# Packed q for the first 512 tokens, weights in 256-column chunks, and a first output stage by chunks of f over four PSUM tiles

## The chip, the core and the metric

The kernel runs on one core of one Trainium2 chip. TensorE (PE) does the matmuls, with its weight loads (PEld) beside them; VectorE (DVE), ScalarE (ACT) and GpSimd (POOL) do elementwise work; SyncE (SP) issues all DMA transfers, in program order. Each engine works through its own instruction list in order and waits on semaphores. Matmul results land in PSUM, eight banks of 128 partitions x 2 KB; all else lives in SBUF, 128 partitions wide. The metric is the device time of one execution, in microseconds; less is better.

## The reference

Decayed linear attention in blocks, four batches, eight heads, 768 tokens, head dimension 64, and then a bilinear feed-forward over the 3072 tokens:

```python
for b in range(nb):
    intra = np.einsum('bhic,bhjc->bhij', qb, kb) * Dmask[None]
    intra = np.einsum('bhij,bhjd->bhid', intra, vb)
    inter = np.einsum('bhid,bhde->bhie', qb * lam_pow[None], kv_state)
    out[:, :, sl] = intra + inter
    kv_state = lam_block[None, :, None, None] * kv_state + np.einsum('bhsd,bhse->bhde', kb_dec, vb)
x = np.ascontiguousarray(attn_out.transpose(0, 2, 1, 3)).reshape(B * S, H * D)   # 3072 x 512
a = x @ w_a          # 512 x 1536
b = x @ w_b          # 512 x 1536
return (a * b @ w_out).astype(np.float32)                                       # 1536 x 512
```

All inputs and the output are float32; the kernel multiplies in bfloat16 and accumulates in float32.

## The kernel before

**Units and groups.** The 3072 tokens are 24 units of 128 tokens (6 units to a batch, `NB = 6`). Units are gathered in groups of `GROUPS = (4, 2, 4, 4, 4, 4, 2)`. The attention of a unit writes 128 columns of its group's `xT` (512 features on 4 x 128 partitions, up to 512 tokens); then `ffn` runs over the group.

**The attention of a unit** is cut in pieces. `prep` scales q and k by powers of lambda (`lp_q`, `lp_k`, made at the start from `lam`) into the bf16 tile `qk` and casts v to `vb`. T (`piece_T`) transposes `qk` on PE into `tps`, eight 128x128 transposes, and copies it to `qkT` on ACT. From unit 10 on (`DMA_T_FROM = 10`) a DMA transpose that SP issues in `prep` fills `qkT` instead. K (`scores`, `masks`) makes the 8 score matrices `kq` and multiplies them by a triangular mask on DVE into `m`. O (`piece_O`) adds the state's part (`o_ps` from `st` and `qkT`) and the masked scores' part (`o_ps` from `m` and `vb`), copies `o_ps` to `xT` on ACT, adds the unit's k and v to the state (`kvd`) and copies the state to `st` on DVE. X is O of a unit with K of the next one inside it.

**ffn** first runs over the 12 chunks f of 128 hidden features: four matmuls into `a_ps` (L306), a copy to `a_sb` on ACT (L309), four matmuls into `b_ps` (L312), and the product `ab` on DVE (L314). Then, for each unit t of the group, 12 matmuls into `op` (L319), a copy to `o_sb` on ACT and a store (L325).

**Hooks.** After each f, and twice in each t, `ffn` calls `hook(slot)`; slots 0 to 11 are the f, 12 and up the halves of the t. The hook emits the next group's attention pieces at the slots that `piece_plan(g)` lists, so PE has them between matmuls of the present group. There is no scheduler: the order of emission is the order on every engine.

**Weights and loads.** `w_a` and `w_b` come in column chunks of 256, 256, 512 and 512 (`W_CHUNKS`), `w_out` in three chunks of 512 rows (o0, o1, o2), all into the staging tiles `wst` (6 buffers), and are cast to bf16 on DVE (`w_a`), ACT (`w_b`) and POOL or DVE (`w_out`). The q, k and v of a unit are three loads of 256 KB in rows of 256 bytes; six units may be loaded ahead (`LOOKAHEAD`). `prefetch` issues them from the hook. SP's order is: `lam`; q, k, v of units 0 to 3 with the first `w_a` and `w_b` chunks between; the other `w_a` and `w_b`; `w_out`; units 4 and 5; then the units one by one, with the stores and DMA transposes where the hooks emit them. The framework lets eight transfers be outstanding: each waits for the one eight places ahead of it.

**The start** (L337 to L351) runs prep and T of unit `step`, K of the unit before and O of the one before that, for six steps, ahead of the first `ffn`. PSUM tiles rotate through seven banks (`ps_bank`); the eighth holds the state.

Of the kernel before, what the change touches and what calls it, by code (L numbers as in the profile page):

```python
# [28 lines left out]
W_CHUNKS = (256, 256, 512, 512)  # L29
LOOKAHEAD = 6  # L30
DMA_T_FROM = 10


def piece_plan(g):

    if g + 1 == len(GROUPS):
        return {}
    if g == 0:  # L40
        ps = [("T", 0, 14), ("K", 0, 15), ("T", 1, 15), ("O", 0, 17), ("K", 1, 17), ("O", 1, 18)]
    elif g == 1:
        ps = [("T", 0, 1), ("K", 0, 3), ("O", 0, 5), ("T", 1, 6), ("K", 1, 8), ("T", 2, 10),
              ("O", 1, 10), ("K", 2, 11), ("O", 2, 12), ("T", 3, 13), ("K", 3, 14), ("O", 3, 15)]
    elif GROUPS[g + 1] == 2:
        ps = [("T", 1, 3), ("X", 0, 5), ("O", 1, 11)]
    else:
        ps = [("T", 1, 2), ("X", 0, 4), ("T", 2, 7), ("X", 1, 9), ("T", 3, 11), ("X", 2, 13),
              ("T", 4, 15), ("X", 3, 17)]
        if g == 2:  # L50
            ps = [("T", 0, 0), ("K", 0, 2)] + ps
    plan = {}
    for name, k, s in ps:
        plan.setdefault(s, []).append((name, k))
    return plan
# [3 lines left out]
def kernel(  # L59
# [19 lines left out]
    assert sum(GROUPS) == NU  # L79
# [5 lines left out]
    wst_pool = ctx.enter_context(tc.tile_pool(name="wst", bufs=6))  # L85
# [4 lines left out]
    st_pool = ctx.enter_context(tc.tile_pool(name="st", bufs=2))  # L90
# [4 lines left out]
    ps_pool = ctx.enter_context(tc.tile_pool(name="ps", bufs=7, space=PSUM))  # L95
# [4 lines left out]
    def ps_bank(name, shape, dt):  # L100
        return ps_pool.tile(shape, dt, name=name, tag="ps")
# [7 lines left out]
    def load_unit(u, which="qkv"):  # L109
        b, nb = divmod(u, NB)  # L110
        for w in which:
            t = ld_pool.tile([128, H, D], F32, name=w + "f", tag=w + "f")
            nc.sync.dma_start(out=t, in_={"q": qr, "k": kr, "v": vr}[w][b, nb])  # L113
            raw[u, w] = t
# [7 lines left out]
    w_off = [sum(W_CHUNKS[:i]) for i in range(len(W_CHUNKS) + 1)]  # L122
    staged = {}

    def load_w(kind, c):
        w = W_CHUNKS[c] if kind != "o" else 512
        t = wst_pool.tile([128, 4, 512], F32, name="wst", tag="wst")
        if kind == "o":
            nc.sync.dma_start(out=t, in_=wo_r[:, 4 * c:4 * c + 4, :])
        else:  # L130
            r = wa_r if kind == "a" else wb_r
            nc.sync.dma_start(out=t[:, :, :w], in_=r[:, :, w_off[c]:w_off[c] + w])
        staged[kind, c] = t

    def cast_w(kind, c, eng):
        t = staged.pop((kind, c))
        if kind == "o":
            dst, src = wo_sb[:, 4 * c:4 * c + 4, :], t
        else:
            w = W_CHUNKS[c]  # L140
            dst = (wa_sb if kind == "a" else wb_sb)[:, :, w_off[c]:w_off[c] + w]
            src = t[:, :, :w]
        if eng == "act":
            nc.scalar.copy(dst, src)
        elif eng == "dve":
            nc.vector.tensor_copy(dst, src)
        else:
            nc.gpsimd.tensor_copy(dst, src)  # L148
# [4 lines left out]
    load_unit(0)  # L153
    load_unit(1)
    load_unit(2, "qk")
    load_unit(3, "qk")
    load_w("a", 0)
    load_unit(2, "v")
    load_unit(3, "v")
    load_w("b", 0)  # L160
    for c in (1, 2):
        load_w("a", c)
        load_w("b", c)
# [4 lines left out]
    gpos = singles.tile([128, NB], F32, name="gpos")  # L168
    nc.gpsimd.iota(gpos, pattern=[[BLK, NB]], base=1, channel_multiplier=1,
# [11 lines left out]
    tmpe = singles.tile([128, NB, H], F32, name="tmpe")  # L181
    lp_q = singles.tile([128, NB, H, 1], F32, name="lp_q")
    lp_k = singles.tile([128, NB, H, 1], F32, name="lp_k")
    nc.vector.tensor_mul(tmpe, _bc(loglam, [loglam.ap[0], [0, NB], loglam.ap[1]]),
                         _bc(gpos, [gpos.ap[0], gpos.ap[1], [0, H]]))
    nc.scalar.activation(lp_q[:, :, :, 0], tmpe, AF.Exp)
    nc.scalar.activation(lp_k[:, :, :, 0], tmpe, AF.Exp, scale=-1.0)
# [7 lines left out]
    def prep_v(u, early):  # L195
        vb = prep_pool.tile([128, H, D], BF16, name="vb", tag="vb")
        vf = raw.pop((u, "v"))
        if early:
            nc.scalar.copy(vb, vf)
        else:  # L200
            nc.vector.tensor_copy(vb, vf)  # L201
        U[u]["vb"] = vb

    def prep(u, early=False):
        nb = u % NB
        qf, kf = raw.pop((u, "q")), raw.pop((u, "k"))
        qk = prep_pool.tile([128, 2, H, D], BF16, name="qk", tag="qk")
        lq = lp_q[:, nb].to_broadcast([128, H, D])
        lk = lp_k[:, nb].to_broadcast([128, H, D])
        (nc.vector if early else nc.gpsimd).tensor_mul(qk[:, 0], qf, lq)  # L210
        nc.gpsimd.tensor_mul(qk[:, 1], kf, lk)  # L211
        U[u] = dict(qk=qk)
        if not early:
            prep_v(u, False)
        if u >= DMA_T_FROM:
            qkT = qkT_pool.tile([128, 2, HP, 128], BF16, name="qkT", tag="qkT")
            nc.sync.dma_start_transpose(out=qkT[:].rearrange("p j hp i -> p (j hp) i"),
                                        in_=qk[:].rearrange("p j h d -> p (j h d)"))
            U[u]["qkT"] = qkT

    def piece_T(u):
        d = U[u]
        if "qkT" in d:
            return
# [6 lines left out]
        d["qkT"] = qkT  # L231

    def scores(u):
        d = U[u]
        qkT = d["qkT"]
        kq = [ps_bank(f"kq{i}", [128, HP, 128], F32) for i in range(2)]
        for hp in range(HP):
            for i in range(2):
                p = slice(64 * i, 64 * i + 64)
                nc.tensor.matmul(kq[i][:, hp, :], lhsT=qkT[p, 1, hp, :], rhs=qkT[p, 0, hp, :],  # L240
# [9 lines left out]

    def piece_K(u):
        masks(u, scores(u))

    def piece_O(u, xT, col, nxt=None):
        nb = u % NB
        d = U.pop(u)
        qk, vb, qkT, m = d["qk"], d["vb"], d["qkT"], d["m"]
        o_ps = ps_bank("o_ps", [128, HP, 128], F32)
        if nb > 0:
            for hp in range(HP):  # L260
                nc.tensor.matmul(o_ps[:, hp, :], lhsT=kv["st"][:, hp, :], rhs=qkT[:, 0, hp, :],  # L261
                                 start=(hp == 0), stop=False, skip_group_check=True)

        def kv_update():
            if nb == NB - 1:
                return
            if nb == 0:
                kv["ps"] = kvps_pool.tile([128, HP, 128], F32, name="kvd", tag="kvd")
            for hp in range(HP):
                nc.tensor.matmul(kv["ps"][:, hp, :], lhsT=qk[:, 1, 2 * hp:2 * hp + 2, :],  # L270
                                 rhs=vb[:, 2 * hp:2 * hp + 2, :],
                                 start=(nb == 0 and hp == 0), stop=True, skip_group_check=True)

        def kv_copy():
            if nb == NB - 1:
                return
            kv["st"] = st_pool.tile([128, HP, 128], BF16, name="st", tag="st")
            nc.vector.tensor_mul(kv["st"], kv["ps"], bdiag_bc)  # L278

        kq = None  # L280
        if nxt is not None:
            kv_update()
            kq = scores(nxt)
        for hp in range(HP):
            for i in range(2):
                p = slice(64 * i, 64 * i + 64)
                nc.tensor.matmul(o_ps[p, hp, :], lhsT=vb[:, 2 * hp + i, :], rhs=m[i][:, hp, :],  # L287
                                 start=(nb == 0 and hp == 0), stop=True, skip_group_check=True)
        nc.scalar.copy(xT[:, :, col:col + BLK], o_ps)  # L289
        if nxt is None:  # L290
            kv_update()
        else:
            masks(nxt, kq)
        kv_copy()
# [4 lines left out]
    def ffn(u0, n, xT, hook):  # L299
        gt = n * BLK  # L300
        ab = ab_pool.tile([128, FC, 512], BF16, name="ab", tag="ab")
        for f in range(FC):
            fsl = slice(f * 128, (f + 1) * 128)
            a_ps = ps_bank("a_ps", [128, 512], F32)
            for s in range(KS):
                nc.tensor.matmul(a_ps[:, :gt], lhsT=wa_sb[:, s, fsl], rhs=xT[:, s, :gt],  # L306
                                 start=(s == 0), stop=(s == KS - 1))
            a_sb = a_pool.tile([128, 512], BF16, name="a_sb", tag="a")
            nc.scalar.copy(a_sb[:, :gt], a_ps[:, :gt])  # L309
            b_ps = ps_bank("b_ps", [128, 512], F32)  # L310
            for s in range(KS):
                nc.tensor.matmul(b_ps[:, :gt], lhsT=wb_sb[:, s, fsl], rhs=xT[:, s, :gt],  # L312
                                 start=(s == 0), stop=(s == KS - 1))
            nc.vector.tensor_mul(ab[:, f, :gt], a_sb[:, :gt], b_ps[:, :gt])  # L314
            hook(f)
        for t in range(n):
            op = ps_bank("op", [128, d_model], F32)
            for f in range(FC):
                nc.tensor.matmul(op, lhsT=ab[:, f, t * 128:(t + 1) * 128], rhs=wo_sb[:, f, :],  # L319
                                 start=(f == 0), stop=(f == FC - 1))  # L320
                if f == FC // 2 - 1:
                    hook(FC + 2 * t)
# [118 lines left out]
```

## Time and profile before

| | us |
|---|---|
| median of 3 runs | 250.44 (250.28 to 252.15) |
| profiled execution, its own time | 251.43 |
| its span, first to last instruction | 249.7 |
| PE busy | 225.8 (90%) |
| DVE, ACT, POOL busy | 111.8, 93.3, 50.5 |
| first FFN matmul | 25.99 |
| FFN of group 0: a and b; output stage | 26.0 to 47.4; 47.4 to 61.5 |
| group 1 | 61.5 to 85.4 |
| DMA: 38.29 MB in 99072 packets | 90368 of them under 512 bytes |

The stage times are read from the timeline: a stage begins with its first matmul. The profile is of one execution, which took 1.0 us more than the median; its instructions' span is 1.7 us less than its time. In lines of the timeline the columns are start (us), duration (us; of several instructions together where a count x follows), engine, line, operation, output and inputs, and in brackets the idle time of the engine just before and what ended it. SPq stands for SP's issuing of transfers: a long one means that the queue could not take it sooner. PE's busy time is modelled, and the four matmuls of a 128x512 quartet, 0.86 us apart from the next quartet, show as 1.03.

### The profile page before, as it was taken

How to read it: one execution, taken by the hardware profiler on the slowest of the kernel's cores; microseconds unless marked ns; L12 is line 12 of the kernel's file. 1: busy time of each engine (PE TensorE's matmuls, PEld its weight loads, DVE VectorE, ACT ScalarE, POOL GpSimd, SP SyncE). 2: the span in 40 equal slices, each digit the busy share in tenths (PEclk: the TensorE clock that was granted, in tenths of full speed). 3: DMA queues.
4: the chain of work that ended last, by engine and by line, in shares of the span. 5: the costliest groups of instructions: out<-in, count | busy, mean ns of one | idle time of the engine just before them, and what ended most of it. 6: DMA issues, size and time to landing. Idle time of an engine off the chain costs nothing.

```text
span 249.7 us, 4045 instructions
## 1 busy us (share of the span) xinstructions
PE 225.8 (90%) x1560; PEld 120.8 (48%) x1584; DVE 111.8 (45%) x182; ACT 93.3 (37%) x157; POOL 50.5 (20%) x56
## 2 busy tenths in 40 slices
PE   0448999999998969999999999999999999999994
PEld 0225444455885424444545455444544545445871
DVE  1166455543666344754326473236463346410430
ACT  5336555263553511332233232233222333222421
POOL 2340006346335400503303063003020000000000
PEclk9999999999999997999999999999999999999999
DMA  6999999999999999992959853270007220002102
GB/s 128 218 251 355 383 387 353 186 220 219 199 280 225 219 255 180 229 182 59 223 147 190 133 97 87 84 168 3 0 1 129 85 41 3 0 38 88 45 1 84
DMA packets 99091, 38.54 MB, mean 154 GB/s; under 512 B 90368, under 2 KB 92416, under 8 KB 99072
## 3 DMA queue, kind: packets, MB, share of 16 engines
q1 hardware_dynamic: 99072, 38.29, 70.4%
q8 instruction: 12, 0.20, 0.3%
q14 instruction: 7, 0.06, 0.1%
HBM read 28.32 MB, written 6.29 MB: 139 GB/s over the span
## 4 chain that ended last, share of the span: by engine, by line
PE 78%; SPq 7%; DMA 7%; DVE 3%; issue 2%; ACT 1%; POOL 1%; DVEq 0%
PE op L319 24%; PE a_ps L306 22%; PE b_ps L312 21%; SPq L113 6%; PE kq L240 3%; PE o_ps L287 3%; DMA qf<-in_q_dram 3%; DMA kf<-in_k_dram 2%; PE tps L228 2%; DMA qkT<-qk 2%; PE kvd L270 2%; PE o_ps L261 2%; DVE m L248 1%; POOL qk L211 1%; SPq L325 1%
## 5 line engine op out<-in xcount | busy, mean ns | idle before, releaser
L314 DVE TENSOR_TENSOR ab<-a_sb,b_ps 128x512 bf16<-128x512 bf16 (+1 forms) x84 | 51.2, 611 | 81.6 <-PE b_ps L312 63.9
L306 PE MATMUL a_ps<-xT,wa_sb 128*128 128x512 bf16 (+1 forms) x325 | 75.7, 350 | 1.8 <-ACT xT L289 0.7
L312 PE MATMUL b_ps<-xT,wb_sb 128*128 128x512 bf16 (+1 forms) x336 | 76.7, 351 | 0.2
L309 ACT CAST a_sb<-a_ps 128x512 bf16<-128x512 f32 (+1 forms) x84 | 44.2, 526 | 70.1 <-PE a_ps L306 65.5
L319 PE MATMUL op<-wo_sb,ab 128*128 128x512 bf16 x275 | 64.7, 379 | 1.1 <-issue 0.3
L312 PEld LDWEIGHTS <-wb_sb 128*128 128x128 bf16 x336 | 33.1, 99 | 30.0 <-issue 1.1
L306 PEld LDWEIGHTS <-wa_sb 128*128 128x128 bf16 x336 | 31.9, 98 | 30.8 <-issue 2.0
L248 DVE TENSOR_TENSOR m<-kq,lotri 128x512 bf16<-128x512 f32 x48 | 30.8, 683 | 33.2 <-PE kq L240 33.2
L319 PEld LDWEIGHTS <-ab 128*128 128x128 bf16 x288 | 27.1, 98 | 31.7 <-issue 0.5
L210 POOL TENSOR_TENSOR qk<-qf,lp_q 128x512 bf16<-128x512 f32 x18 | 19.0, 1054 | 94.7 <-PE kvd L270 34.0
L324 ACT COPY o_sb<-op 128x512 f32<-128x512 f32 x24 | 14.1, 586 | 45.7 <-PE op L319 43.7
L211 POOL TENSOR_TENSOR qk<-kf,lp_k 128x512 bf16<-128x512 f32 x24 | 25.8, 1075 | 13.9 <-DMA kf<-in_k_dram 13.7
L289 ACT CAST xT<-o_ps 128x512 bf16<-128x512 f32 x24 | 14.1, 586 | 20.3 <-PE o_ps L287 20.2
L228 PE MATMUL tps<-ident,qk 128*128 128x128 bf16 x80 | 8.3, 255 | 12.9 <-DVE qk L210 11.1
L278 DVE TENSOR_TENSOR st<-kvd,bdiag 128x512 bf16<-128x512 f32 x20 | 13.7, 684 | 7.1 <-PE kvd L270 7.1
L230 ACT COPY qkT<-tps 128x1024 bf16<-128x1024 bf16 x10 | 10.1, 1012 | 11.5 <-PE tps L228 11.5
L228 PEld LDWEIGHTS <-qk 128*128 128x128 bf16 x80 | 5.9, 112 | 15.1 <-DVE qk L210 11.9
L240 PE MATMUL kq<-qkT 64*128 64x128 bf16 x192 | 10.3, 231 | 2.3 <-DMA qkT<-qk 2.3
L287 PE MATMUL o_ps<-m,vb 128*64 128x128 bf16 x192 | 10.6, 232 | 0.7 <-DVE m L248 0.7
L201 DVE CAST vb<-vf 128x512 bf16<-128x512 f32 x18 | 10.3, 574 | 0.0
L148 POOL CAST wo_sb<-wst 128x2048 bf16<-128x2048 f32 x2 | 4.8, 2402 | 22.7 <-DMA wst<-in_moe_w_out_dram 22.7
L261 PE MATMUL o_ps<-qkT,st 128*128 128x128 bf16 x80 | 8.0, 224 | 1.2 <-DVE st L278 1.2
(28 smaller groups left out, 56.8 us busy)
## 6 DMA issues: line engine op xcount, KB each, us to landing
qf<-in_q_dram SPq DMA_DIRECT2D x24, 256.0 KB, 4.9
kf<-in_k_dram SPq DMA_DIRECT2D x24, 256.0 KB, 5.0
vf<-in_v_dram SPq DMA_DIRECT2D x24, 256.0 KB, 4.9
out_dram<-o_sb SPq DMA_DIRECT2D x24, 256.0 KB, 2.2
wst<-in_moe_w_out_dram SPq DMA_DIRECT2D x3, 1024.0 KB, 11.6
wst<-in_moe_w_a_dram SPq DMA_DIRECT2D x2, 1024.0 KB, 12.1
wst<-in_moe_w_b_dram SPq DMA_DIRECT2D x2, 1024.0 KB, 13.1
wst<-in_moe_w_a_dram SPq DMA_DIRECT2D x2, 512.0 KB, 5.6
```

The lines of the kernel that those rows point to most:

```text
L113: nc.sync.dma_start(out=t, in_={"q": qr, "k": kr, "v": vr}[w][b, nb])
L210: (nc.vector if early else nc.gpsimd).tensor_mul(qk[:, 0], qf, lq)
L211: nc.gpsimd.tensor_mul(qk[:, 1], kf, lk)
L228: nc.tensor.transpose(tps[:, j, hp, :], d["qk"][:, j, 2 * hp:2 * hp + 2, :], ident)
L240: nc.tensor.matmul(kq[i][:, hp, :], lhsT=qkT[p, 1, hp, :], rhs=qkT[p, 0, hp, :], start=True, stop=True, skip_group_check=True)
L248: nc.vector.tensor_mul(m, kq[i], lotri_bc)
L287: nc.tensor.matmul(o_ps[p, hp, :], lhsT=vb[:, 2 * hp + i, :], rhs=m[i][:, hp, :], start=(nb == 0 and hp == 0), stop=True, skip_group_check ...
L306: nc.tensor.matmul(a_ps[:, :gt], lhsT=wa_sb[:, s, fsl], rhs=xT[:, s, :gt], start=(s == 0), stop=(s == KS - 1))
L309: nc.scalar.copy(a_sb[:, :gt], a_ps[:, :gt])
L312: nc.tensor.matmul(b_ps[:, :gt], lhsT=wb_sb[:, s, fsl], rhs=xT[:, s, :gt], start=(s == 0), stop=(s == KS - 1))
L314: nc.vector.tensor_mul(ab[:, f, :gt], a_sb[:, :gt], b_ps[:, :gt])
L319: nc.tensor.matmul(op, lhsT=ab[:, f, t * 128:(t + 1) * 128], rhs=wo_sb[:, f, :], start=(f == 0), stop=(f == FC - 1))
```

## The change

1. **Packed q.** For units 0 to 3 (the first 512 tokens of batch 0) q is loaded as `q4`, four consecutive tokens to a partition, in two transfers with rows of 1 KB. Two DVE multiplies scale it (`lp_q` gets four more columns, with positions in this packing), 16 transposes and two ACT copies put it back in token order in `qT4`. Units 0 to 3 transpose only k (`transpose_k`). `qs4` and `qT4` borrow an `ab` buffer.
2. **Start by hand.** The loop over steps becomes a written list of pieces; state update and copy (`kv_update`, `kv_copy`) of unit 3 move into group 0's slot 0. The state copy of unit 2 goes to ACT, v of units 2 and 3 to POOL. `st` becomes two fixed tiles, set to zero once.
3. **Weights.** `w_a` and `w_b` come in six chunks of 256 columns, staged in eight buffers; `w_out` chunks use a pool `big` of two buffers, which they share with `q4`. A list `pending` fixes the order of all loads, and `pump`, called after each cast and in each `prep`, issues as many as buffers allow. All `w_out` casts are on DVE, at slots 10, 14 and 18.
4. **Group 0.** `ffn` makes two `a` and then two `b` (`FW = 2`). The output stage runs chunk by chunk: four f at a time for each of four `op` tiles, which hold four banks; its slots are 12 to 23.
5. **Plans.** The preps have their own entries P, most a slot earlier than before; that of unit 10 moves from group 2's slot 0 to group 1's slot 13, and its K from slot 2 to slot 1.
6. **End.** The last unit's `op` is made in column pieces of 256, 128 and 128, each copied and stored by itself.

By the changed kernel's instruction lists, SP's order is: `lam`; `q4` in two; k and v of units 0 to 3; twelve weight chunks; o0; unit 4; o1; unit 5; o2; units 6 to 11; the four stores of group 0; units 12 to 15; the first store of group 1; unit 16; the DMA transpose of unit 10; the other store of group 1; unit 17; the transpose of unit 11; and so on, a unit's loads and a transpose in turn. The load of o2 waits for DVE's cast of o0. On DVE group 0 runs: product of f = 0, copy of the state, cast of `w_a` chunk 1, product of f = 1, product of f = 2, cast of chunk 2, product of f = 3, and so on to product of f = 10, cast of o0, q and v of unit 4, product of f = 11.

```diff
-W_CHUNKS = (256, 256, 512, 512)
+W_COLS = 256
+W_BUFS = 8
+PACK = 4
...
     if g == 0:
-        ps = [("T", 0, 14), ("K", 0, 15), ("T", 1, 15), ("O", 0, 17), ("K", 1, 17), ("O", 1, 18)]
+        ps = [("P", 0, 10), ("T", 0, 12), ("K", 0, 13), ("O", 0, 15),
+              ("P", 1, 15), ("T", 1, 17), ("K", 1, 18), ("O", 1, 20)]
     elif g == 1:
-        ps = [("T", 0, 1), ("K", 0, 3), ("O", 0, 5), ("T", 1, 6), ("K", 1, 8), ("T", 2, 10),
-              ("O", 1, 10), ("K", 2, 11), ("O", 2, 12), ("T", 3, 13), ("K", 3, 14), ("O", 3, 15)]
+        ps = [("P", 0, 0), ("T", 0, 1), ("K", 0, 3), ("P", 1, 4), ("O", 0, 5), ("T", 1, 6),
+              ("P", 2, 7), ("K", 1, 8), ("T", 2, 9), ("P", 3, 9), ("O", 1, 10), ("K", 2, 11),
+              ("O", 2, 12), ("T", 3, 13), ("P", 4, 13), ("K", 3, 14), ("O", 3, 15)]
...
         if g == 2:
-            ps = [("T", 0, 0), ("K", 0, 2)] + ps
+            ps = [("K", 0, 1)] + ps
...
+    def ps_bank(name, shape, dt, hold=False):
+        i = bank["next"]
+        while i in bank["held"]:
+            i = (i + 1) % 7
+        bank["next"] = (i + 1) % 7
...
+    pending = [("a", 0), ("b", 0)]
+    for c in range(1, NWC):
+        pending += [("a", c), ("b", c)]
+    n0 = GROUPS[0]
+    pending += [("o", 0), ("q", n0), ("k", n0), ("v", n0), ("o", 1),
+                ("q", n0 + 1), ("k", n0 + 1), ("v", n0 + 1), ("o", 2)]
+    for u in range(n0 + 2, NU):
+        pending += [("q", u), ("k", u), ("v", u)]
+    def pump():
+        while pending:
+            kind, c = pending[0]
+            if kind == "o":
+                if sum(1 for x in staged if x[0] == "o") >= 2:
+                    return
+            elif kind in "ab":
+                if sum(1 for x in staged if x[0] != "o") >= W_BUFS:
+                    return
+            elif c >= used["u"] + LOOKAHEAD:
+                return
+            pending.pop(0)
...
+    q4 = big_pool.tile([128, H, PACK, D], F32, name="q4", tag="big")
+    q4_r = q[0, :, 0:PACK * BLK, :].rearrange("h (p r) d -> p h (r d)", r=PACK)
+    for i in range(2):
+        hs = slice(4 * i, 4 * i + 4)
+        nc.sync.dma_start(out=q4[:, hs].rearrange("p h r d -> p h (r d)"), in_=q4_r[:, hs])
...
     def prep(u, early=False):
+        make_ks(u, "pool")
+        make_qs(u, "dve" if early else "pool")
+        make_vb(u, "dve")
+        used["u"] = u + 1
+        pump()
         if u >= DMA_T_FROM:
...
+        if first:
+            for f0 in range(0, FC, FW):
+                a_sbs = [a_part(f, xT, gt) for f in range(f0, f0 + FW)]
+                for f in range(f0, f0 + FW):
+                    b_part(f, xT, gt, a_sbs[f - f0], ab)
+                    hook(f)
+            ops = [ps_bank("op", [128, d_model], F32, hold=True) for _ in range(n)]
+            slot = FC
+            for c in range(NWO):
+                for t in range(n):
+                    out_mms(ops[t], ab, t, range(4 * c, 4 * c + 4))
+                    if c == NWO - 1:
+                        store(u0 + t, ops[t], 0, d_model)
+                    hook(slot)
+                    slot += 1
...
+            if last and t == n - 1:
+                for lo, hi in ((0, 256), (256, 384), (384, 512)):
+                    if lo:
+                        op = ps_bank("op", [128, d_model], F32)
+                    out_mms(op, ab, t, range(FC), lo, hi)
+                    store(u0 + t, op, lo, hi)
...
+        nc.vector.tensor_mul(qs4[:, :, hs, :].rearrange("p r h d -> p h r d"), q4[:, hs],
+                             lp_q[:, NB:, hs, :].rearrange("p r h o -> p h r o")
+                             .to_broadcast([128, 4, PACK, D]))
+        tps = ps_bank("tq", [128, 2, PACK, 128], BF16)
+        for j in range(2):
+            for r in range(PACK):
+                h = 4 * i + 2 * j
+                nc.tensor.transpose(tps[:, j, r, :], qs4[:, r, h:h + 2, :], ident)
+        nc.scalar.copy(qT4[:, 2 * i:2 * i + 2, :].rearrange("c hp (p r) -> c hp r p", r=PACK), tps)
...
             if g == 0:
                 if slot == 0:
+                    kv_update(3)
+                    kv_copy(3)
+                if slot % FW == 0 and slot // FW + 1 < NWC:
+                    cast_w("a", slot // FW + 1, "dve")
+                if slot % FW == 1 and slot // FW + 1 < NWC:
+                    cast_w("b", slot // FW + 1, "act")
+                if slot == 10:
+                    cast_w("o", 0, "dve")
+                if slot == 14:
+                    cast_w("o", 1, "dve")
+                if slot == 18:
+                    cast_w("o", 2, "dve")
```

## The prediction

> **What bounds the kernel now.** I read the page first, its row of busy tenths for PE and for DMA:
>
> ```profile
> PE   0448999999998969999999999999999999999994
> ...
> DMA  6999999999999999992959853270007220002102
> ```
>
> A slice is 6.24 us. PE has three holes: the start (slices 0 to 3), one at slice 14 (87 to 94 us), and the tail. DMA is full from slice 1 to slice 17 (to 112 us). So a transfer in that stretch arrives when the queue gets to it. By stretches of time PE is idle 14.5 us before 26.0 us, 0.6 from 26.0 to 47.4, 0.4 from there to 61.5, 0.8 from there to 85.4, 2.9 between 85 and 96, and 4.0 after 230. Next the hole at slice 14, in the chain that ended last (start, us, what):
>
> ```profile
> 88.97 4.37 DMA qkT<-qk
> 93.39 0.51 PE kq L240 x8
> 93.91 0.54 PE a_ps L306
> ```
>
> PE waits for the first DMA transpose, that of unit 10 (T10 from here on), and every later instruction is behind it. The timeline of SP shows why T10 is issued at 88.97 (start, us, engine, line):
>
> ```profile
> 83.80 1.09 SPq L113 DMA_DIRECT2D qf<-in_q_dram  x1
> 84.98 1.09 SPq L113 DMA_DIRECT2D kf<-in_k_dram  x1
> 86.16 1.09 SPq L113 DMA_DIRECT2D vf<-in_v_dram  x1
> 87.34 1.53 SPq L325 DMA_DIRECT2D out_dram<-o_sb  x2
> 88.97 1.67 SPq L217 DMA_TRANSPOSE qkT<-qk  x1
> ```
>
> SP issues without a pause; a 256 KB load takes it 1.1 us here and 0.57 at 101.43, where the queue is short. T10's place in this list sets its time. Last, the timeline of FFN group 0, how late a DVE cast can come:
>
> ```profile
> 26.85 1.03 PE L312 MATMUL b_ps<-xT,wb_sb 128*128 128x512 bf16 x4
> ...
> 27.98 0.69 DVE L314 TENSOR_TENSOR ab<-a_sb,b_ps 128x512 bf16<-128x512 bf16 x1 [1.61 <-PE b_ps L312]
> ...
> 28.59 0.69 DVE L146 CAST wa_sb<-wst 128x1024 bf16<-128x1024 f32 x1
> ...
> 29.33 0.64 PEld L306 LDWEIGHTS <-wa_sb 128*128 128x128 bf16 x4 [0.22 <-DVE wa_sb L146]
> ```
>
> From the start of a `b_ps` quartet it is 1.13 us to DVE's product, 0.61 more to the cast behind it, and 0.74 more to the weight load that needs it: 2.48 us.
>
> **Start, to the first FFN matmul (25.99 before).** Removed: four q loads of 256 KB in 256-byte rows, four DVE multiplies, 16 transposes of q. Added: two q loads of 512 KB in 1 KB rows, two multiplies of 128x1024, 16 transposes, two ACT copies. Bytes move at 216 to 223 GB/s where only q, k and v flow (6 to 15 us) and at 386 where weights flow in long rows (30 to 39 us). So q's 1.05 MB take 2.7 us instead of 4.8: the queue gains 2.0 us. The chain: `lp_q` ready at 5.5; two multiplies, each twice the 0.68 of 128x512, to 8.3; eight cold transposes to ACT's start 1.13 (18.71 to 19.84) and a copy of 1.01 to 10.5; the k copy, about 0.56, to 11.1; scores to masks 0.71 and two masks 1.29: 13.1. Units 1 to 3 each add the same pair on DVE with a state copy, a k transpose or a score wait between: masks end at 15.7, 18.7 and 20.5. Then 0.65 to ACT, 0.59 for `xT`: FFN starts at S = 22.0. Two more memsets and two casts of v on POOL (some 1.0 each, as its L211) end before their units are due. Bounds: 20 if the units follow at 2.4 us, 24 if the strided multiply and copy of the packed q take twice their time. The gain is 4.0 us.
>
> **FFN group 0 (21.4 us before).** The order is now a, a, b, b for two f, and the cast of the next `wa` chunk stands on DVE behind the product of the first f. The next chunk therefore starts 1.73 (two a quartets) + 2.48 = 4.21 us after the last, against 3.45 of PE work: 0.76 lost at each of five borders, 0.4 more at the first, where `kv_copy(3)` goes ahead. Sum 4.2 us. The `wb` casts on ACT (1.04) have a whole a pair for cover; without it they would cost up to 1.04 each. The last chunk starts at S + 21.7. Now `wo`'s cast o0 comes on DVE behind the product of f = 10: 1.13 + 0.61 + 1.22 after that b quartet, so it ends at S + 26.4 = 48.4, and the first `op` matmul waits 1.3 us for it. Behind o0 on DVE stand unit 4's q and v (0.69, 0.42) and the last product; T of unit 4, one t later, finds them done. Before, POOL had cast o0 from 39.44.
>
> **First out stage (14.2 us before).** The same 48 matmuls and pieces. T to K has one t (0.86) in place of six matmuls (1.29) for cover, so 0.5 us is lost twice. Casts o1 and o2 (1.22 each) stand ahead of or beside masks and are covered by two t. With o0: 16.1 us. Group 0 ends at S + 41.2 = 63.2, 1.7 later than before. Holding four PSUM banks leaves three: tps, two kq and o_ps reuse banks two pieces old; I cost that at 0, up to 0.5.
>
> **The queue, which decides.** By order o2 is the third user of two big buffers, so SP waits for cast o0 (48.4) before it can issue o2, and the loads of unit 6 and all after stand behind it. All ahead of o2 has landed by about 46.9: before, unit 5's v was there by 51.6 (ACT's cast of it), less o2's 2.7 and q's 2.0. (The last four weight pieces wait for casts from S on, to about S + 5, with four pieces or more, 1.4 us each, still queued ahead: 0.) So DMA runs dry for 2 to 4 us. An out store lands 2.2 us after its issue with 0.7 us of data, so a dry queue needs 1.5; then 1 MB at 386 GB/s, 2.7; then q6, 1.2: 53.8. Before it landed at 53.2 (POOL's wait for it ends there). If the old queue's lag of about 2.5 us of landing behind throughput stays, it is up to 3.2 later. So +0.6 to +3.2; I take +1.0, since the queue starts empty. T10 now goes out in group 1's slot 13, before its old place by program (group 2's slot 0). But `prep` calls `pump` first: T10 stands behind unit 16's three loads (3.5 us), and one out store (0.8, half of the 1.53 above) is gone from ahead of it. T10 lands at 93.3 + 1.0 + 3.5 - 0.8 = 97.0. Low end 93.6: +0.6, and 11 units at 3.29 (SP's three from 77.46 to 87.34) where POOL's waits for q show 3.56 (53.21 to 63.87). High end 101: the lag, and all units at 3.56. PE reaches K0, now slot 1, at 63.2 + 23.9 + 0.3 + 3.45 = 90.9 and waits about 6 us instead of 2.3. After T10 the rest is PE's: K0 came at 93.39 and now at 97.05, +3.7, with one f more behind it (two quartets, 1.73). T11 needs a store, three loads and its own data, 6.2 us after T10; its scores come 7.6 after (K0 0.3, three f 5.2, a cold 1.5, other pieces 0.6), so I cost it at 0 (up to 1).
>
> **Tail.** ACT's last copy shrinks from 0.59 to about 0.27 (128x256 took 0.37), the last store from 256 to 64 KB: -0.3 to -0.85, I take -0.6.
>
> **Sum:** +3.7 + 1.7 - 0.6 = +4.8. On the profiled execution's 251.43 (span 249.7) it gives 256.2. That run is 1.0 above the median of 250.44, which gives **255.2**. The start's 4.0 and the losses of group 0 enter only through cast o0.
>
> **Two rules beside it.** After a 2.31 us wait at 93.39 matmuls went at 0.43 us instead of 0.216 until 96.8, 1.5 us lost; after 0.79 us of idling at 24.57 they did not slow, and from 22.7 to 26.0 PE idled about a third and stayed fast. So five waits of 0.76 cost only themselves. "TensorE: Matmul & The Clock Gate" of the Trainium skill, "A second HAM failure mode", says that frequent short idling between groups makes the clock oscillate. By that rule group 0's 20.7 us of a and b could double, cast o0 would come up to 20 us later, and the time be near 275; no row before shows it.
>
> Weights in 512 KB pieces: bytes went at 357 GB/s at 21 to 24 us and at 386 at 30 to 36, where pieces are 1 MB; for 6.3 MB that is 1.3 us at most, inside the dry time. "DMA: Bandwidth & Descriptors", section "Bandwidth", speaks against smaller pieces: it advises batches of 1 MiB or more, with 138 GB/s at 64 KB and 341 at 1 MB. At a middle 240 (an estimate from that page) the weights would take 26 us instead of 16 and delay every load behind them; the row of 357 does not agree.
>
> **Rivals.** A, on the other side: T10 lands before PE is there (90.9). Then K0 starts 2.5 earlier, one f more is left, and the cold 1.5 and tail 0.6 are saved: -2.9, 247.5. For it: some units went at 3.29 us, and q is cheaper. Against: DMA is full to 112 us and T10 has a unit more ahead. The point is a T10 that lands 6 us before my 97.0. B: the cast waits or the gate do not bind (cast o0 by 45). Then q6 lands about 2 us before its old time, T10 at 94.0, time about 252.3. C: T10 at its late end (+4.0) with T11's 1 and the banks' 0.5: 260.7, and each us that a slower clock adds to group 0 comes on top. D, the change does not do what it says: the packed q saves nothing, S = 24 to 26, cast o0 is 2 to 4 us later: 257 to 259, within the forecast's range.
>
> **How the numbers follow.** Forecast with D 0.56 (252 to 260), A 0.16, B 0.20, C 0.08. A measurement here tells 1%, 2.5 us, from no change. A gives 0.11 to faster and 0.05 to same; B 0.15 to same, 0.05 to slower; the forecast 0.03 to same. Sum 0.11, 0.23, 0.66. The range, 248 to 260, leaves out half of A and C and a little of the forecast.
>
> **What would show it.** FFN from 22; waits of `a_ps` on DVE's `wa_sb` of about 0.8 five times; a dry DMA slice near 48; unit 10's scores waiting about 6 us for `qkT<-qk`. Wrong: no such wait, or T10 issued before 85.

## The result, and the profile after

The changed kernel takes 261.37 us (258.97 to 261.88, four runs) beside 251.18 (250.28 to 252.15, four runs) for the one before: the ratio is 1.039, 95% interval 1.031 to 1.047. It is slower, by 10.2 us where 4.8 were forecast, and lies outside the forecast range of 248 to 260. The profiled execution took 261.88, the longest of the four, with a span of 260.2 (before 249.7, so +10.5).

First the page of the changed kernel: its rows of busy tenths, 6.5 us to a slice.

```profile
PE   0397888889999943999999999999999999999995
...
PEclk9999999999999995799999999999999999999999
DMA  5999998569999999948828675235021230002102
GB/s 177 222 288 349 329 302 222 131 207 220 217 215 288 226 240 241 172 86 177 184 81 172 114 163 119 83 97 104 3 42 43 81 81 3 0 0 93 71 1 82
```

The hole of slice 14 is still there, it is wider (slices 14 and 15, 91 to 104 us), and the granted clock falls in its second half and behind it (0.5 in slice 15, 0.7 in slice 16). DMA has a new hole at slice 7 (45.5 to 52 us, 131 GB/s), which the queue before did not have. Then the chain that ended last, at the hole (start, us, what):

```profile
92.10 0.88 PE a_ps L382 x4
92.98 0.02 issue
93.00 0.59 ACT a_sb L389
93.60 0.03 issue
93.62 1.09 SPq L399
...
97.68 4.30 DMA qkT<-qk
101.98 0.05 issue
102.02 0.61 PE kq L298 x8
102.63 1.82 PE a_ps L382 x4
```

It is the same hand-over as before: T10 lands, K0 starts. K0 came at 93.39 before and comes at 102.02 now, 8.6 later. From K0 to the end of the span it is 158.2 us where it was 156.3. PE had reached K0 at 93.8; the waits of PE show what it lost there and in group 0 (who waits for whom: us in total, times, longest):

```profile
PE kq L298 <- DMA qkT<-qk: 8.2, 1, 8.2
...
PE a_ps L382 <- DVE wa_sb L159: 3.6, 5, 1.0
...
PE op L403 <- DVE wo_sb L159: 1.1, 1, 1.1
```

Five waits at the chunk borders and one at the out stage are there as predicted, but they total 4.7 us, and PE still came 8.2 us early. Why T10 is late is read from the timeline of SP (start, us, engine, line):

```profile
42.20 4.78 SPq L126 DMA_DIRECT2D vf<-in_v_dram  x1
52.81 0.37 SPq L143 DMA_DIRECT2D wbig<-in_moe_w_out_dram  x1
...
93.62 1.09 SPq L399 DMA_DIRECT2D out_dram<-o_sb  x1
94.81 0.39 SPq L126 DMA_DIRECT2D qf<-in_q_dram  x1
95.25 0.81 SPq L126 DMA_DIRECT2D kf<-in_k_dram  x1
96.15 1.43 SPq L126 DMA_DIRECT2D vf<-in_v_dram  x1
97.68 2.15 SPq L268 DMA_TRANSPOSE qkT<-qk  x1
```

SP issues nothing from 47.0 to 52.81: it stands at o2, until DVE has cast o0 out of one of the two big buffers. By windows of 4 us the transfers move 68 GB/s from 48 to 52. At the other end stand a store, unit 16's three loads and then T10. Now the start, from the timeline of ACT, PE and DVE (the bracket is the idle time before and what ended it):

```profile
7.89 4.70 ACT L467 COPY scratch<-tq 128x1024 bf16<-128x1024 bf16 x2 [2.25 <-PE tq L466]
...
20.48 0.61 PE L298 MATMUL kq<-scratch,qkT 64*128 64x128 bf16 x8 [0.31 <-ACT qkT L289]
...
24.32 0.59 PE L382 MATMUL a_ps<-xT,wa_sb 128*128 128x512 bf16 x1 [0.68 <-ACT xT L329]
25.12 2.77 PE L382 MATMUL a_ps<-xT,wa_sb 128*128 128x512 bf16 x6 [0.22 <-issue]
27.68 1.47 PE L382 MATMUL b_ps<-xT,wb_sb 128*128 128x512 bf16 x4
...
31.20 1.90 PE L382 MATMUL a_ps<-xT,wa_sb 128*128 128x512 bf16 x8 [0.97 <-DVE wa_sb L159]
...
34.08 0.69 DVE L394 TENSOR_TENSOR ab<-a_sb,b_ps 128x512 bf16<-128x512 bf16 x1 [2.33 <-PE b_ps L382]
34.68 0.69 DVE L159 CAST wa_sb<-wst 128x1024 bf16<-128x1024 f32 x1
...
35.42 0.55 PEld L382 LDWEIGHTS <-wa_sb 128*128 128x128 bf16 x4 [1.08 <-DVE wa_sb L159]
...
51.56 1.22 DVE L159 CAST wo_sb<-wbig 128x2048 bf16<-128x2048 f32 x1
```

The two copies of packed q take 4.70 us together, 2.35 each, where the sum had 1.01 each. FFN starts at 24.32. Six of its first eight `a` matmuls, in the line from 25.12 on, take 2.77 us, 0.43 apart where later ones are 0.216 apart: PE is at half clock, or cold, until about 28.9. The first chunk therefore runs from 24.32 to 31.20, 6.88 us; the next start at 35.43, 39.65, 43.87 and 48.09, every 4.2. The last line is DVE's cast of o0, which ends at 52.78; SP issues o2 at 52.81.

### The profile page after: what moved, and what is told of

Same layout as the page of the kernel before. It is cut to its first block, busy times and chain, and to the rows that moved or that the text cites. A ratio compares the mean times of both kernels' runs of the same rounds, so it can differ in the third digit from the quotient of the medians.

```text
span 260.2 us, 4121 instructions
## 1 busy us (share of the span) xinstructions
PE 229.5 (88%) x1584; PEld 123.7 (48%) x1608; DVE 112.2 (43%) x186; ACT 95.5 (37%) x161; POOL 46.7 (18%) x58
## 4 chain that ended last, share of the span: by engine, by line
PE 83%; ACT 6%; DVE 4%; DMA 3%; issue 2%; SPq 1%; DVEq 0%; ACTq 0%
PE a_ps L382 26%; PE op L403 23%; PE b_ps L382 22%; PE kq L298 3%; PE o_ps L322 3%; PE kvd L341 2%; ACT scratch L467 2%; DMA qkT<-qk 2%; PE o_ps L314 2%; DVE ab L394 1%; DVE wa_sb L159 1%; DMA lam_sb<-in_lam_dram 1%; PE tps L278 1%; SPq L126 1%; ACT qkT L280 1%
## 5 line engine op out<-in xcount | busy, mean ns | idle before, releaser
L382 PE MATMUL a_ps<-xT,wa_sb 128*128 128x512 bf16 (+1 forms) x328 | 77.5, 359 | 5.2 <-DVE wa_sb L159 3.6
L403 PE MATMUL op<-wo_sb,ab 128*128 128x512 bf16 (+2 forms) x299 | 64.9, 362 | 2.0 <-DVE wo_sb L159 1.1
L243 POOL TENSOR_TENSOR qk<-kf,lp_k 128x512 bf16<-128x512 f32 x23 | 24.3, 1059 | 145.3 <-issue 46.8
L398 ACT COPY o_sb<-op 128x512 f32<-128x512 f32 (+2 forms) x26 | 14.4, 553 | 45.7 <-PE op L403 43.7
L298 PE MATMUL kq<-qkT 64*128 64x128 bf16 x160 | 8.2, 223 | 8.7 <-DMA qkT<-qk 8.2
L298 PEld LDWEIGHTS <-qkT 64*128 64x128 bf16 x192 | 6.0, 101 | 17.1 <-DMA qkT<-qk 8.7
L280 ACT COPY qkT<-tps 128x1024 bf16<-128x1024 bf16 x6 | 6.1, 1013 | 7.2 <-PE tps L278 7.2
L466 PE MATMUL tq<-ident,scratch 128*128 128x128 bf16 x16 | 2.1, 311 | 7.4 <-DVE scratch L459 7.4
L341 PE MATMUL kvd<-vb,qk 128*128 128x128 bf16 x80 | 8.4, 233 | 0.1
L314 PEld LDWEIGHTS <-st 128*128 128x128 bf16 x80 | 6.4, 104 | 4.5 <-ACT st L352 0.5
```

Source lines behind the costliest of these rows:

```text
L243: eng_of(eng).tensor_mul(qk[:, 1], raw.pop((u, "k")), lp_k[:, u % NB].to_broadcast([128, H, D]))
L298: nc.tensor.matmul(kq[i][:, hp, :], lhsT=d["kT"][p, hp, :], rhs=d["qT"][p, hp, :], start=True, stop=True, skip_group_check=True)
L341: nc.tensor.matmul(kv["ps"][:, hp, :, :], lhsT=d["qk"][:, 1, 2 * hp:2 * hp + 2, :], rhs=d["vb"][:, 2 * hp:2 * hp + 2, :], start=(nb == 0 a ...
L382: nc.tensor.matmul(ps[:, :gt], lhsT=w_sb[:, s, f * 128:(f + 1) * 128], rhs=xT[:, s, :gt], start=(s == 0), stop=(s == KS - 1))
L398: nc.scalar.copy(o_sb[:, lo:hi], op[:, lo:hi])
L403: nc.tensor.matmul(op[:, lo:hi], lhsT=ab[:, f, t * 128:(t + 1) * 128], rhs=wo_sb[:, f, lo:hi], start=(f == 0), stop=(f == FC - 1))
```

## The experiments

Two theories. **The queue theory**: the end is set by T10, T10 by its place on SP, and that queue's clock by o2, hence by the cast of o0. What shortens the way to that cast, frees o2 from it, or takes loads from ahead of T10 moves the end; what PE wins elsewhere only lengthens its wait. **The PE theory**, its rival: the loss is PE's own work and waits in group 0 and in the new out stage, and the wait for T10 would shrink with them or stay harmless. Each experiment is the changed kernel with the edit shown, unless it says otherwise. "o2" and "T10" are the times at which SP issues them; 52.81 and 97.68 in the changed kernel. A difference of 2 to 3 us between two sets of four runs is near their scatter: the ratio's interval of the changed kernel, 1.031 to 1.047, overlaps those of every run below with a ratio of 1.026 to 1.030. There the times in the traces carry the argument, each of one execution.

### T10 ahead of unit 16's loads

```diff
-        used["u"] = u + 1
-        pump()
         if u >= DMA_T_FROM:
             ...
+        used["u"] = u + 1
+        pump()
```

> prep issues the DMA transpose before it calls pump, so unit 10's transpose goes out ahead of unit 16's three loads; nothing else changes. Queue theory (the time follows when unit 10's transpose lands, at 102.0 in the changed kernel): it lands 3.5 us earlier, near 98.5, the wait of unit 10's scores falls from 8.2 to about 4.7, and the time by 3.5 us to about 258. PE theory (each us that PE loses in the start and group 0 is lost at the end, the transpose's wait is only a part of it that would come back elsewhere): within 1 us of 261.4.

258.74 (257.0 to 259.34), ratio 1.028: 2.6 less. T10 went out at 95.08, 2.60 earlier (o2 was 0.4 later in this trace), and PE's wait for it fell from 8.2 to 4.9. PE's own work is untouched, so this is the worth of the place alone, where the PE theory allowed 1 us. It is less than the 3.5 of three loads at 1.1 us, since the queue is short at that place and the three take 0.39 to 1.43.

### Three big buffers

```diff
-tc.tile_pool(name="big", bufs=2)
+tc.tile_pool(name="big", bufs=3)
-                if sum(1 for x in staged if x[0] == "o") >= 2:
+                if sum(1 for x in staged if x[0] == "o") >= 3:
```

> The big pool has three buffers, so the load of o2 no longer waits for DVE's cast of o0, and the loads of unit 6 and later follow unit 5 at once. PE's work, its order and all casts stay. Queue theory: unit 5's loads are through near 50.5 and o2 no longer starts at 54.3, so unit 10's transpose lands 3.5 to 4 us earlier, near 98, and the time falls by as much, to 257.5. PE theory: group 0 still ends at 67.1, so the time stays within 1 us of 261.4.

255.18 (254.09 to 257.63), ratio 1.017: 6.2 less. The timeline of SP and then the timeline of PE in this run:

```profile
45.09 0.92 SPq L143 DMA_DIRECT2D wbig<-in_moe_w_out_dram  x1
...
91.73 2.12 SPq L268 DMA_TRANSPOSE qkT<-qk  x1
```

```profile
96.11 0.40 PE L298 MATMUL kq<-qkT 64*128 64x128 bf16 x8 [1.17 <-DMA qkT<-qk]
```

o2 no longer waits for the cast, T10 is issued 5.95 earlier, and K0 waits 1.17 us. K0 comes 5.9 earlier, more than the expected 4. After so short a wait the eight score matmuls take 0.40, against 0.61 behind the wait of 8.2: the clock has not fallen, and from K0 to the end it is 156.3 us in place of 158.2. This profiled execution, the quickest of its four (254.09), is thus 7.8 shorter by its span. PE's 3.3 us at the borders (3.6 in the changed kernel) and its 1.1 at the out stage are still there, so they did not cost the time directly.

### The old order a, b, a, b in group 0

```diff
-            for f0 in range(0, FC, FW):
-                a_sbs = [a_part(f, xT, gt) for f in range(f0, f0 + FW)]
-                for f in range(f0, f0 + FW):
-                    b_part(f, xT, gt, a_sbs[f - f0], ab)
-                    hook(f)
+            for f in range(FC):
+                a_sb = a_part(f, xT, gt)
+                b_part(f, xT, gt, a_sb, ab)
+                hook(f)
```

> Group 0 makes a, b, a, b again, one f at a time; the hooks and casts keep their slots. The cast of the next w_a chunk then has one f of cover, so the five waits of a_ps for wa_sb (3.6 us in all, with the last of PE's queue 4.2) should go. Cast o0 comes about 4 us earlier, near 48.5. Queue theory: loads of unit 5 are through near 50.5 and become what o2 waits for in place of the cast; the transpose of unit 10 lands 3 to 4 us earlier and the wait of its scores stays about 8 us, since PE is there 4 us earlier too; time about 257.5. PE theory: also -4 us, but then with the wait of the scores below 5 us.

257.81 (257.03 to 258.59), ratio 1.026: 3.6 less. None of PE's matmuls waits for `wa_sb` any more, o2 goes out at 48.60 and T10 at 93.58. PE wins its 3.6 and waits as long as ever:

```profile
PE kq L298 <- DMA qkT<-qk: 8.3, 1, 8.3
```

The border waits count, but through the cast of o0: both ends of the wait moved by some 4 us.

### Packed q copied with a contiguous write

```diff
-        nc.scalar.copy(qT4[:, 2 * i:2 * i + 2, :].rearrange("c hp (p r) -> c hp r p", r=PACK), tps)
+        nc.scalar.copy(qT4[:, 2 * i:2 * i + 2, :].rearrange("c hp (p r) -> c hp p r", r=PACK),
+                       tps[:].rearrange("c hp r p -> c hp p r"))
```

> The two ACT copies of the packed q (2.35 us each, against 1.01 for the same 128x1024 before) read PSUM with a stride and write SBUF without one. If the strided bf16 write is what costs, each takes about 1.0 and FFN starts 2.7 us earlier, at 21.6; cast o0 and the time come 2.5 us earlier (about 259). If a strided read costs as much, nothing changes. Whether PE's clock has risen by the first FFN matmul may shift this by 2 us either way.

258.62 (258.38 to 259.41), ratio 1.030: 2.75 less. The timeline of ACT has the same elements, read with a stride from PSUM and written in order:

```profile
7.83 1.01 ACT L467 COPY scratch<-tq 128x1024 bf16<-128x1024 bf16 x1 [2.25 <-PE tq L466]
9.34 1.01 ACT L467 COPY scratch<-tq 128x1024 bf16<-128x1024 bf16 x1 [0.50 <-PE tq L466]
```

So 1.01 is the price when SBUF is written in order, and 2.35 when every fourth bf16 is written. FFN starts at 22.14, against the 22.0 of the prediction. PE is still at half clock there, and the first chunk takes 6.50 us. o2 moves to 50.25, T10 to 95.67.

### A warm PE at the first chunk

```diff
     transpose_k(0)
+    warm = ps_bank("warm", [128, 4, 128], BF16)
+    for i in range(36):
+        nc.tensor.transpose(warm[:, i % 4, :], ident, ident)
```

> The changed kernel with 36 more transposes of the identity on PE after unit 0's k transposes, where PE waits 3.2 us for ACT; their result is not read. In the changed kernel the first seven quartet-halves of FFN run at 0.43 us a matmul and chunk 0 takes 6.9 us instead of 4.8. If PE's clock rises with its share of busy time, it now rises before FFN starts at about 24: chunk 0 takes 4.8, cast o0 comes 2 us earlier, and by the queue theory the time is 2 us less, about 259.3. If the clock does not depend on this, the time stays at 261.4.

259.11 (258.21 to 259.59), ratio 1.029: 2.3 less. The timeline of PE:

```profile
9.55 3.64 PE L477 MATMUL warm<-ident 128*128 128x128 bf16 x36
13.12 0.40 PE L298 MATMUL kq<-scratch,qkT 64*128 64x128 bf16 x8
...
22.27 1.89 PE L382 MATMUL a_ps<-xT,wa_sb 128*128 128x512 bf16 x8 [0.68 <-ACT xT L329]
```

After 36 transposes of the identity, whose result nothing reads, PE is at full clock from 13.12 (0.40 for eight score matmuls; 0.61 in the changed kernel up to 20.48). FFN starts at 22.27, 2.05 earlier although the two copies still take 4.72, since PE's pieces of the start are shorter too. The first chunk takes 4.80 us in place of 6.88; the prediction's sum leaves 4.9 for it. o2 goes out at 48.68, 4.13 earlier, but T10 only 3.05 earlier.

### Both terms of the start

The two edits above together.

> Both terms of the start undone together: the ACT copies of packed q write contiguously, and 36 identity transposes warm PE before FFN. Alone they brought -2.75 and -2.3. If the start reaches the end only through the cast of o0 they add: FFN starts near 20, the cast of o0 ends near 46.2, o2 is issued then, the transpose of unit 10 near 92.8, and the time is 256.4 (255 to 257.5). If the DMA queue is not dry any more by 46, so that the cast of o0 stops deciding, the second of them is worth less: 257.5 to 258.5.

258.18 (257.17 to 259.7), ratio 1.027: 3.2 less where 5.0 were expected, a miss. In the profiled execution, the quickest of the four, the terms do not add at the start: FFN starts at 21.15, 3.2 earlier (2.2 and 2.05 alone), and o2 goes out at 47.55, 5.3 earlier (2.6 and 4.1 alone). At T10 they nearly do: it goes out at 92.77, 4.91 earlier (2.01 and 3.05 alone), and the span is 255.5. Why the median gains less stays open, since there is no trace of the longer executions.

### All of these, and the cast of o0 on POOL

The edits of the first four experiments together, and `cast_w("o", 0, "pool")` in place of `"dve"`.

> Five edits of the changed kernel together: the transpose ahead of pump, three big buffers, a b a b in group 0, the packed q copied with a contiguous write, and cast o0 on POOL (which also removes the 1.1 us that the first op matmul waits). PE alone would bring unit 10's scores to 94.9 - 2.2 - 4.0 - 1.1 = 87.6 (94.9 is where PE reaches them with three big buffers). Queue theory: the transpose is then bound by the loads ahead of it, lands near 92, and its wait is back at about 4 us with a cold clock behind it: time near 252. PE theory: 245.5.

252.31 (250.84 to 254.31, ten runs); ratio 1.003, interval 1.000 to 1.006, the same as before. T10 is issued at 89.78, and PE, whose losses in group 0 are gone, still waits 8.0 us for it. That is the queue theory at its plainest, though the trace is that of the longest of the ten (254.31).

### The same, with four units loaded ahead

```diff
-LOOKAHEAD = 6
+LOOKAHEAD = 4
```

> The same five edits and LOOKAHEAD 4 in place of 6: the transpose of unit 10 stands behind unit 13's loads, not unit 15's, 7 us of transfers fewer. Queue theory: it lands near 85, before PE gets to the scores at 87.6; no wait there, time near 246. If instead the loads then come too late for their units (buffers free only when a unit is used), waits for k, q or v appear and the time is no better than with six.

244.08 (243.65 to 244.82); ratio 0.970, interval 0.968 to 0.972. This version beats both kernels. Timeline of SP, and of PE at K0:

```profile
82.38 1.37 SPq L268 DMA_TRANSPOSE qkT<-qk  x1
```

```profile
86.43 0.40 PE L300 MATMUL kq<-qkT 64*128 64x128 bf16 x8 [1.96 <-DMA qkT<-qk]
```

Six loads fewer stand ahead of T10, and it goes out 7.4 us earlier. The time falls by 8.2, the wait of 8.0 to 2.0.

### The same, with three units ahead

> The run that combined all edits and LOOKAHEAD 4 (244.08, longest wait for the transpose of unit 10 2.0 us), with LOOKAHEAD 3: three more loads leave the place ahead of the transpose, it is issued near 79, PE does not wait for it, and the time is 242 to 243. Rival: with three units ahead the loads of a unit come too late for its prep on POOL and DVE, the next transposes are late, and the time is 246 or more.

244.38 (244.03 to 244.88): no better than four, and above the expected 242 to 243; not late either. T10 goes out at 79.70 and nobody waits for it. What it wins is lost at the start of this profiled execution, where FFN begins at 22.08 on a half-clock PE (21.56 at full clock in the run before it). Whether that holds for the other three executions is not shown.

### Only the look-ahead

The changed kernel with `LOOKAHEAD = 4` and no other edit.

> The changed kernel with two units less loaded ahead (LOOKAHEAD 4 in place of 6), nothing else. The transpose of unit 10 then stands behind unit 14's loads instead of unit 16's: six loads of about 1.1 us and perhaps an out store fewer. Queue theory: it is issued near 91 (97.68 in the changed kernel), lands near 95.5, PE waits 1 to 2 us for it, too little to fall to half clock, and the time comes to 255 (as the run with three big buffers, 255.18). If only the first wait moves and the next transposes become late in turn, 258. PE theory (group 0's length sets the time): 261, no change.

252.84 (250.34 to 253.81, nine runs; a tenth took 254.78 and is not counted); ratio 1.003, interval 1.000 to 1.007. This one constant takes back 8.5 of the 10.2 us between the two kernels. From the waits of PE in this run:

```profile
PE a_ps L382 <- DVE wa_sb L159: 3.3, 5, 1.0
PE kq L298 <- DMA qkT<-qk: 1.2, 2, 0.8
PE op L403 <- DVE wo_sb L159: 1.1, 1, 1.1
```

The border waits and o2's wait for the cast (o2 at 51.51) are all still there; T10 goes out at 88.93 instead of 97.68. The profiled execution (251.24) is below the expected 255: K0's wait is 0.8 and the clock holds behind it. Its start was also 0.9 us quicker than the changed kernel's (FFN at 23.45). The timeline of PE shows the clock rise and fall there:

```profile
20.46 0.40 PE L298 MATMUL kq<-scratch,qkT 64*128 64x128 bf16 x8 [0.31 <-ACT qkT L289]
...
23.45 3.55 PE L382 MATMUL a_ps<-xT,wa_sb 128*128 128x512 bf16 x8 [0.68 <-ACT xT L329]
```

The score matmuls are fast at 20.46, where the changed kernel's took 0.61, and the first eight `a` matmuls are at half clock again. From 20.4 to 23.4 PE is busy for 60%, with pauses of 0.68 us at most; from 23.4 to 26.8 the granted clock is 0.51.

### The kernel before, with five units ahead

The kernel before with `LOOKAHEAD = 5`.

> The kernel before with LOOKAHEAD 5 in place of 6 and nothing else: its transpose of unit 10 stands behind unit 14's loads in place of unit 15's. Queue theory: it lands 3.5 us earlier, near 89.8, and PE reaches the scores at 91.1, so the 2.3 us wait goes and with it the 1.5 us of half clock: -3.8, time near 247.3. If the hole at 91 to 97 us had another cause, no change (251).

251.11 (249.16 to 251.59, ten runs); ratio 0.997, interval 0.994 to 1.000: a miss. The wait for T10 is gone and with it the half clock at 95 us, but the span did not shrink (249.4, 249.7 before). The timeline of PE of this run shows a different start:

```profile
21.88 0.61 PE L240 MATMUL kq<-qkT 64*128 64x128 bf16 x8
...
27.09 1.87 PE L306 MATMUL a_ps<-xT,wa_sb 128*128 128x512 bf16 x4
28.75 1.91 PE L312 MATMUL b_ps<-xT,wb_sb 128*128 128x512 bf16 x4
30.45 1.53 PE L306 MATMUL a_ps<-xT,wa_sb 128*128 128x512 bf16 x4
31.82 1.03 PE L312 MATMUL b_ps<-xT,wb_sb 128*128 128x512 bf16 x4
```

In the trace of before the same eight score matmuls took 0.40:

```profile
21.86 0.40 PE L240 MATMUL kq<-qkT 64*128 64x128 bf16 x8
```

PE had become fast there, and here it did so at about 31. Up to that instruction the two traces agree within 0.05 us. Group 2 starts at 89.45 here and at 85.74 before; the 3.7 between them is the gain that is missing. Nor did T10 come earlier, as the timeline of SP shows:

```profile
85.38 3.83 SPq L325 DMA_DIRECT2D out_dram<-o_sb  x2
89.31 1.39 SPq L217 DMA_TRANSPOSE qkT<-qk  x1
```

SP is through with unit 14's loads at 83.0 and then stands at the two stores of group 1, the second of which needs PE's last `op` of that group. So T10 goes out 0.34 later than the 88.97 of before, and the wait is gone because PE is late. In this run T10 is bound by PE's end of group 1, not by the loads.

### The same, with PE kept busy at the start

```diff
         if 0 <= step - 1 < n0:
             piece_K(step - 1)
+        if step in (1, 2):
+            warm = ps_bank("warm", [128, 4, 128], BF16)
+            for i in range(30 if step == 1 else 12):
+                nc.tensor.transpose(warm[:, i % 4, :], ident, ident)
```

> The kernel before with LOOKAHEAD 5 and 42 identity transposes in PE's pauses of the start, so that FFN begins at full clock. If the run without them (251.11) had its gain of about 3.8 at the wait eaten by a cold start of group 0, this one gives 247.3 (246.5 to 248.5), with FFN starting at 26 and quartets 0.86 us apart from the first. If the lost gain has another cause, 250 to 251.

247.69 (246.48 to 248.64); ratio 0.984, interval 0.980 to 0.989. Timeline of PE:

```profile
25.05 1.02 PE L306 MATMUL a_ps<-xT,wa_sb 128*128 128x512 bf16 x4 [0.36 <-ACT xT L289]
25.91 1.03 PE L312 MATMUL b_ps<-xT,wb_sb 128*128 128x512 bf16 x4
```

FFN starts at full clock, T10 goes out at 85.68 and PE does not wait for it. So the miss was the cold start, and the kernel before also pays for T10's place: 1.6% with the two edits. By the two traces the span is 4.7 shorter than before (245.0): PE is at K0 0.7 earlier, 2.3 of waiting is gone, and 1.6 of half clock behind it. No run has the extra transposes alone, so this split rests on those traces.

## Why the prediction was right in its mechanism and wrong in its size

**The bound.** T10 sets the end, by its place on SP: confirmed by moving it (2.6), by the look-ahead (8.5), and by edits to the work ahead of PE's K0 that left its wait at 8.0 to 8.8. PE as its own bound is refuted by the first two experiments and by the old order of a and b.

**Cast o0 gates o2, and o2 the queue.** Confirmed by the third big buffer. From o2's issue to T10's landing the prediction had 48.6 us (48.4 to 97.0); the trace has 49.2 (52.81 to 102.0). From o2's issue to T10's issue it is 44.9 to 46.0 in the five runs in which o2 waits for o0 and nothing behind it is moved. That part of the sum was right as a whole, in some measure by luck: unit 16's loads, put at 3.5, held T10 up for 2.9 (94.81 to 97.68), so other terms, which no run took apart, must have been larger than stated.

**Cast o0's end: the step that failed.** It was put at 48.4 and came at 52.8. Two terms were mis-sized, and both lie before chunk 1. One is S: 24.32 for 22.0, because the copy of packed q was costed by a row that writes in order. (The terms named for S add up to 21.7; 0.3 of the 22.0 is not named.) The text gave 24 as a bound "if the strided multiply and copy of the packed q take twice their time"; the multiplies took their time (1.22 and 1.23), the copies 2.3 times theirs, and the contiguous write gave 22.14. The other is the first chunk, 6.88 us for 4.9 (the 21.7 from S to the last chunk, less four periods of 4.21), because PE was cold: the prediction took the clock at the first FFN matmul from the trace of before, and asked of the clock gate only whether the border waits would trip it. That PE was fast there in that trace was luck: in another execution of the same start it became so at 31. The warmed run gave 4.80. Together the two put cast o0 4.4 us late, and with 0.6 more between o2 and T10 the 97.0 became 102.0. They are not independent: a warm PE alone brought FFN's start to 22.27 as well, and with both undone T10 went out 4.9 earlier.

**After K0.** One f more, less the tail, was put at +1.1 and is +1.9. The tail gained 0.63, as said (8.35 us from the last group's first `op` matmul to the end of the span, 8.98 before). The other 0.8 is the clock: PE is at half clock until 107.4 and loses 2.4 us by it, where after the wait of 2.3 it lost 1.6 until 97.1 (each is the time from K0 to the first fast quartet, less 0.33 for the scores and 0.864 for each quartet between). The sum had not counted this.

In one line of spans: 8.6 at K0 in place of 3.7, and 1.9 in place of 1.1, give +10.5 in place of +4.8. With these terms put right the forecast would have been 255.2 + 4.4 + 0.6 + 0.8 = 261.0, where 261.37 was measured; the late S alone would have left it inside the range.

**The borders and the out stage.** As predicted: period 4.22 (4.21), waits of about 0.7 each, op's wait 1.1 (1.3). From the end of o0's cast to group 1 it is 14.3 us (52.8 to 67.1), where 14.8 were expected (48.4 to 63.2). None of this set the end.

**The two rules.** The clock did not oscillate at the borders: quartets stayed 0.86 us apart, so the 275 of that rule did not come. But the row that the prediction trusted, a third idle and still fast, is no safe one: in the run with only the look-ahead changed 40% idle from 20.4 to 23.4, in pauses of 0.68 us at most, was followed by a granted clock of 0.51. For 512 KB pieces the windows from 20 to 28 us show 349 GB/s, near the 357 taken and far from the 240 of the estimate.

**The rivals.** A and B did not happen. D was right that the start would be late, but it priced S alone; its "within the forecast's range" missed the cold chunk. C had the size (260.7, plus what a slower clock in group 0 adds) with a late T10, but by way of the queue's lag, T11 and the banks rather than the start; at 0.08 it was given too little.

**The start's cold PE, and a rule on it.** "TensorE: Matmul & The Clock Gate" of the Trainium skill, section "The HAM clock gate", says that the clock is released after a window of some 3.4 us of sustained work, that these windows run free, and that one kernel can therefore show different numbers of cold matmuls. The traces agree that the moment varies: the same PE instructions became fast at 21.9 in the trace of before and near 31 in that with five units ahead, and behind 36 unbroken transposes PE was fast (they took 3.64 us in one run and 2.62 in another, so it rose earlier in the second). No run here measures the window. The traces differ from the page in size: it puts the spread at half a microsecond and the cost below 1% of a typical span; here it was 9 us of clock and 3.7 us of 250. That PE's small pauses are the reason (3.18 us busy in the 3.4 from 16.4 in the changed kernel, and still cold) fits the warmed runs, but no run varied the pauses alone.

## What to carry to other kernels

A transfer that issues in order is as early as the slowest buffer that any earlier load of its queue waits for: follow that buffer back to the instruction that frees it, and count every term on the way, the first instructions of the kernel too. How far ahead loads run is a position in that queue, not only a reserve; here one constant was worth 8 us in two versions of the changed kernel. A price for a copy holds for its write pattern, and a price for a matmul for the clock it will meet, so both must be asked of the place where the work is going to stand.

## What was not expected of the hardware

- ACT, bf16 128x1024 from PSUM: 2.35 us when it writes every fourth element of SBUF, 1.01 when it reads with that stride and writes in order.
- PE can stay at half clock for almost 16 us in which it is busy for 88%: in the changed kernel from 13.07 to 28.9. The granted-clock figure stood at 1.00 in all windows of that time, and fell to 0.5 to 0.8 only in and behind the wait of 8.2 us; before its first rise the matmuls' own durations are the only witness.
- A wait of 1.2 us or of 2.0 us at K0 left the clock up (0.40 for eight score matmuls); 2.31 in the kernel before and all longer ones brought it down. At the start, behind less work, pauses of 0.68 us at most were followed by half clock too (0.51 from 23.4 to 26.8 with only the look-ahead changed). Each of these is one execution.
